# Denominators of odd tiles alone on POOL, the others by a square on ACT and a join on DVE, with a planner that keeps POOL and two-operand DVE passes apart

## The chip, the cores and the metric

The kernel runs on one core of a Trainium2 chip. The metric is the device time of one execution in microseconds (us). A core has a matrix engine (PE, with weight loads, PEld, beside it), a vector engine (DVE), an activation engine (ACT), a general engine (POOL) and a queue that issues transfers (SP). Each takes its instructions strictly in the order in which they were written, and waits for semaphores of the others.

## The reference, cut to what matters

Three layers follow each other on 4608 tokens (8 sequences of 576, 8 heads of 64 columns):

```python
p_packed = sm_attn(p, k, v)            # 32 packed rows for each head
x = sm_attn(q, p_packed, p_packed)     # 4608 x 512
h = x @ w_in                           # 512 -> 2048, call it layer 2
P = a[0] + a[1]*h + a[2]*h**2 + a[3]*h**3
Q = 1.0 + np.abs(b[0])*np.abs(h) + np.abs(b[1])*h**2
x = (P / (Q + 1e-6)) @ w_out           # 2048 -> 512
h = x @ w_in2                          # 512 -> 1024, layer 3
solu = h * softmax(h)
out = (layernorm(solu) * g_ln) @ w_out2  # 1024 -> 512
```

The change is about Q, the denominator of layer 2. Weights arrive as 64-bit floats and are turned into 32-bit ones on the chip.

## The kernel before, in words

The tokens go in nine blocks of 512 (j = 0 to 8). A block has 16 tiles of layer 2 (i = 0 to 15), each 128 of the 2048 columns by 512 tokens: `m_h` makes h in PSUM on PE, `elem` makes g = P/Q from it on ACT, POOL and DVE, and `m_y` multiplies g into four PSUM banks that collect the block's y. Blocks 0 and 1 (`NRAW = 2`) run these products in float32; from block 2 on all is split into a high and a low float16 half, with three passes for each product. `y_out` then splits y into `ybig`, and in four groups of 128 tokens `s_h2`, `s_sm`, `s_lt`, `s_ln` and `s_out` do layer 3.

`elem` of one tile, before: ACT takes u = |h| (L690), POOL makes s = |b1| u + |b0| (a tensor_scalar, shown under the helper's line L335 as `s<-u,aba`) and s = s u (a tensor_tensor, L692), so that s = Q - 1. ACT makes the start of P (L693), DVE two passes on it that read h from PSUM (L694, L695), ACT the logarithm and the exponential of s as a first reciprocal (L696, L697), DVE one Newton step and the product (L698, L699, and L701 in blocks 0 and 1 or L703 after). From block 2 on ACT rounds g to float16 (L704) and POOL makes the low half (L705, `g<-B,g`).

Ahead of this stands the start. `w_decode` turns 24 groups of weights into float32 with three DVE passes each (L399, L400, L401), ACT takes absolute values (L408) for bounds, PE sums those with a matrix of ones, and `w_split` (L457 on ACT, L458 on DVE) makes float16 halves. The attention of the next batch element runs between the tiles: `a_s1`, `a_tr`, `a_pp` (PE, with DVE's `p` pass, L332, behind it), `a_pt` (L518), `a_s2` and `a_pw`, which makes four groups of `pw` (PE into a pair of PSUM banks, ACT L538, DVE L539). The same pair of banks, the slot "S2", also serves `s_h2`, whose last reader is DVE's L757.

The order on every engine is made while the program is built. Each piece of work is a part of `plan` with an engine, a due time, a cost, and the keys that it reads and writes. `Plan.order` walks through a pretended execution: whenever an engine is free in it, the ready part with the earliest due time is taken, within `DUE["ahead"]` of the pace of the `m_h` parts. The due time of a part is 16 j + DUE[name] + offset, and a key (j, name) in `DUE` takes the place of the bare name. On the chip nothing of this clock is left: only each engine's order and the semaphores are.

## Time and profile before

| | before |
|---|---|
| median of 3 runs | 1197.74 us (1196.11 to 1203.66) |
| the profiled execution | 1202.27 us, its span 1200.4 us |
| PE busy | 1115.8 us, 93% |
| DVE busy | 976.8 us, 81% |
| ACT busy | 762.0 us, 63% |
| POOL busy | 706.3 us, 59% |
| TensorE clock granted, mean | 0.983 |

The span runs from the first to the last instruction. The busy time of an engine is the part of the span in which it has an instruction at work; register, branch and semaphore instructions don't count. An average over the span mixes a start, in which weights are decoded, with a long even stretch and an end, so the rows below are read by stretch.

### The profile page before, as it was taken

Reading aid. Unit: us, or ns where it says so; the run is one execution under the profiler, and the core shown is the slowest. Engines: PE = TensorE matmul, PEld = TensorE weight load, DVE = VectorE, ACT = ScalarE, POOL = GpSimd, SP = SyncE. Lnnn points to the kernel's source line nnn. Section 1 sums busy time; section 2 is a strip of 40 time slices with the busy share of each in tenths; the row PEclk is TensorE's granted clock in tenths of the full one; section 3 lists DMA queues with packets and bytes.
Section 4 is the critical chain, followed back from the end, with each engine's and each line's share of the span. In section 5 each row is a group of like instructions: output and inputs, shape, how many; then the busy total and the mean of one; then the engine's idle time right before and its main releaser. Section 6 shows DMA issues by size and latency. Waiting matters only on the chain.

```text
span 1200.4 us, 17951 instructions
## 1 busy us (share of the span) xinstructions
PE 1115.8 (93%) x6549; PEld 529.7 (44%) x6550; DVE 976.8 (81%) x1477; ACT 762.0 (63%) x1256; POOL 706.3 (59%) x931
## 2 busy tenths in 40 slices
PE   4678989999999999999999998999999999999998
PEld 1133344444444454444544454444444444444443
DVE  5987999999978978888878887888788886788633
ACT  3556666676856667567756766577656666667624
POOL 0163847554658647676666655765675865867612
PEclk9698999999999999999999999999999999999999
DMA  9664033110222121311231114111311121211123
GB/s 342 224 230 161 7 123 99 36 53 1 54 77 67 27 54 55 88 27 28 62 109 27 27 40 131 27 27 27 117 28 27 27 53 28 53 27 27 27 53 88
DMA packets 108120, 83.54 MB, mean 70 GB/s; under 512 B 78208, under 2 KB 88576, under 8 KB 108032
## 3 DMA queue, kind: packets, MB, share of 16 engines
q1 hardware_dynamic: 108032, 82.40, 24.4%
q8 instruction: 51, 0.84, 0.3%
q14 instruction: 37, 0.30, 0.1%
HBM read 54.07 MB, written 9.44 MB: 53 GB/s over the span
## 4 chain that ended last, share of the span: by engine, by line
PE 47%; DVE 23%; POOL 13%; ACT 9%; issue 5%; DMA 2%; SPq 0%; DVEq 0%; ACTq 0%; POOLq 0%
PE P L329 37%; PE h L329 9%; POOL s L692 4%; POOL cf L335 3%; DVE B L699 3%; POOL s L335 2%; DVE s L698 2%; POOL g L705 2%; ACT u L696 2%; DVE B L694 2%; DVE B L695 2%; POOL d L335 1%; DVE w L401 1%; DMA lbig<-lbig 1%; DVE at L629 1%
## 5 line engine op out<-in xcount | busy, mean ns | idle before, releaser
L329 PE MATMUL P<-g,w 128*128 128x512 f16 (+1 forms) x1600 | 423.4, 414 | 0.7 <-DVE ybig L729 0.7
L329 PE MATMUL h<-at,pw 128*128 128x192 f16 (+11 forms) x1408 | 235.4, 315 | 8.3 <-ACT at L646 3.2
L335 POOL TENSOR_SCALAR s<-u,aba 128x512 f32<-128x512 f32 x130 | 137.6, 1058 | 173.7 <-ACT u L690 150.9
L329 PEld LDWEIGHTS <-w 128*128 128x128 f16 x1440 | 138.4, 98 | 167.5 <-issue 12.1
L329 PE MATMUL P<-w,ybig 128*128 128x512 f16 x864 | 193.9, 381 | 9.0 <-DVE pw L539 2.5
L705 POOL TENSOR_TENSOR g<-B,g 128x512 f16<-128x512 f32 x112 | 144.2, 1287 | 80.9 <-ACT g L704 76.6
L692 POOL TENSOR_TENSOR s<-s,u 128x512 f32<-128x512 f32 x130 | 186.3, 1433 | 7.0
L329 PE MATMUL P<-w,lbig 128*128 128x512 f16 x768 | 173.0, 379 | 4.9 <-DVE pw L539 2.9
L335 POOL TENSOR_SCALAR d<-d 128x1 f32<-128x1 f32 x216 | 85.3, 395 | 156.6 <-ACT E L790 73.1
L696 ACT ACTIVATE u<-s,lnb 128x512 f32<-128x512 f32 x130 | 93.8, 721 | 98.4 <-POOL s L692 97.9
L698 DVE SCALAR_TENSOR_TENSOR s<-s,u 128x512 f32<-128x512 f32 x130 | 109.2, 840 | 47.8 <-ACT u L697 47.0
L329 PEld LDWEIGHTS <-ybig 128*128 128x128 f16 x864 | 84.7, 98 | 114.2 <-issue 16.0
L329 PEld LDWEIGHTS <-pw 128*128 128x128 f16 x1152 | 101.6, 98 | 64.5 <-issue 13.3
L329 PEld LDWEIGHTS <-lbig 128*128 128x128 f16 x768 | 74.6, 98 | 92.6 <-issue 8.1
L694 DVE SCALAR_TENSOR_TENSOR B<-h,cf,B 128x512 f32<-128x512 f32 x112 | 83.0, 741 | 27.5 <-ACT B L693 27.3
L693 ACT ACTIVATE B<-h,cf 128x512 f32<-128x512 f32 x112 | 86.6, 773 | 21.5 <-POOL g L705 21.5
L699 DVE SCALAR_TENSOR_TENSOR B<-B,cf,u 128x512 f32<-128x512 f32 x101 | 98.2, 972 | 0.0
L697 ACT ACTIVATE u<-u,lnb 128x512 f32<-128x512 f32 x133 | 95.6, 719 | 2.0
L690 ACT ACTIVATE u<-h,cf 128x512 f32<-128x512 f32 x101 | 68.9, 682 | 39.9 <-PE h L329 38.1
L695 DVE SCALAR_TENSOR_TENSOR B<-B,cf,h 128x512 f32<-128x512 f32 x112 | 82.8, 739 | 1.5
L704 ACT CAST g<-B 128x512 f16<-128x512 f32 x112 | 68.6, 613 | 21.6 <-PE P L329 16.9
L703 DVE SCALAR_TENSOR_TENSOR B<-s,B 128x512 f32<-128x512 f32 x98 | 81.0, 827 | 1.1
(144 smaller groups left out, 1469.3 us busy)
## 6 DMA issues: line engine op xcount, KB each, us to landing
w<-in_w_in_dram SPq DMA_DIRECT2D x10, 1024.0 KB, 9.2
kq<-in_kT_dram SPq DMA_DIRECT2D x8, 1152.0 KB, 6.2
w<-in_w_out_dram SPq DMA_DIRECT2D x9, 1024.0 KB, 8.1
kq<-in_qT_dram SPq DMA_DIRECT2D x9, 1024.0 KB, 5.4
out_dram<-w SPq DMA_DIRECT2D x36, 256.0 KB, 2.4
v<-in_vN_dram SPq DMA_DIRECT2D x15, 512.0 KB, 3.7
lbig<-in_w_out_dram SPq DMA_DIRECT2D x3, 1024.0 KB, 5.4
lbig<-in_w_in_dram SPq DMA_DIRECT2D x2, 1024.0 KB, 7.0
```

The costliest lines, as they stand in the source:

```text
L329: nc.tensor.matmul(out=o, lhsT=lhsT, rhs=rhs, start=start, stop=stop)
L335: gp.tensor_scalar(out=o, in0=i, scalar1=s1, scalar2=s2, op0=o0, **({"op1": o1} if o1 else {}))
L692: pool(due, c_pool(512, 2), lambda: gp.tensor_tensor(out=T(s_), in0=T(s_), in1=T(u_), op=ALU.mult), [u_, s_], [s_])
L693: sc(due, c_act(512, 163), lambda: act.activation(out=T(B_), in_=T(h_), func=AF.Identity, scale=coef(17), bias=coef(16)), [h_, *R], [B_], ...
L694: dve(due, c_dve(512), lambda: stt(out=T(B_), in0=T(h_), scalar=coef(14), in1=T(B_), op0=ALU.mult, op1=ALU.mult), [h_, B_, *R], [B_])
L695: dve(due, c_dve(512), lambda: stt(out=T(B_), in0=T(B_), scalar=coef(15), in1=T(h_), op0=ALU.subtract, op1=ALU.mult), [h_, B_, *R], [B_])
L696: sc(due, c_act(512, 105), lambda: act.activation(out=T(u_), in_=T(s_), func=AF.Ln, scale=2.0 ** -40, bias=lnb[:, 0:1]), [s_, "lnb"], [u_])
L697: sc(due, c_act(512, 105), lambda: act.activation(out=T(u_), in_=T(u_), func=AF.Exp, scale=-1.0, bias=lnb[:, 1:2]), [u_, "lnb"], [u_])
L698: dve(due, c_dve(512, 140), lambda: stt(out=T(s_), in0=T(s_), scalar=1.0 + 1e-6, in1=T(u_), op0=ALU.add, op1=ALU.mult), [s_, u_], [s_])
L699: dve(due, c_dve(512, 240), lambda: stt(out=T(B_), in0=T(B_), scalar=coef(18), in1=T(u_), op0=ALU.subtract, op1=ALU.mult), [B_, u_, *R], [B_])
L703: dve(due, c_dve(512, 95), lambda: stt(out=T(B_), in0=T(s_), scalar=2.0, in1=T(B_), op0=ALU.subtract, op1=ALU.mult), [s_, B_], [B_])
L705: pool(due, (1250, 1290), lambda: gp.tensor_tensor(out=T(g_)[:, 1, :], in0=T(B_), in1=T(g_)[:, 0, :], op=ALU.subtract), [B_, g_], [g_])
```

## The change: what it does

1. `elem` has two ways to Q. For odd tiles of blocks 2 to 8 (`Q_POOL`) all stays. For the other tiles (all 32 of blocks 0 and 1, and 56 of the later ones) ACT makes s = (c h)^2 and u = |b0 c h|, and one DVE pass joins them, s = |b1| s + u. The coefficient c b0 is a new small POOL instruction for each block (C(22)).
2. Parts on POOL, and DVE passes marked `port=True` (those with two operands in SBUF, and the decode's first), may not overlap in the pretended execution: while one of them is at work, `Plan.order` holds the others back. No semaphore is added for that.
3. Planner's costs: lower ones for POOL (`c_pool`, `SMALL_P`, L705's), and the extra time that some DVE passes had been given is taken out.
4. `DUE` gets due times for each group of loads and decodes (L00 to D33) and separate ones for blocks 0, 1 and 8, with new numbers everywhere; `ahead` goes from 14.05 to 25.54.

`LOW_POOL` is 0 for every matrix and `LO_POOL` is always true, so those two branches change nothing.

```diff
 DUE = {
-    "ahead": 14.05, "misc": -33.52, "L0": -86.47, "L1": 5.38, "D0": -129.29, "D1": -37.47, "L2": 15.2, "L3": -131.81, "D2": 27.27, "D3": 30.75,
+    "ahead": 25.54, "misc": -68.19, "S1": -126.89, "S2": -106.52, "S3": -44.43, "bound": -35.99, "mean": -76.81, "k": -7.86, "v": -59.3,
...
-    def add(self, eng, due, cost, fn, r=(), w=(), new=(), pace=None):
+    def add(self, eng, due, cost, fn, r=(), w=(), new=(), pace=None, port=False):
...
+        if port or eng == "POOL":
+            self.port.add(n)
...
                         due, n = heapq.heappop(heap)
+                        if n in self.port and port_at > now:
+                            held.append((due, n))
+                            continue
...
                     free_at[eng] = now + occ
+                    if got in self.port:
+                        port_at = now + occ
...
+    LOW_POOL = {1: 0, 2: 0, 3: 0}
+    Q_POOL = lambda j, i: j > 1 and i % 2
+    LO_POOL = lambda j, i: True
...
-        lat = (2.4 * n + 220) if tensors > 1 else (1.3 * n + 330)
+        lat = (2.14 * n + 175) if tensors > 1 else (0.94 * n + 290)
...
             steps += [("p", C(15), C(14), C(12), None, ALU.mult),
+                      ("p", C(22), C(14), abc[:, 4:5], None, ALU.mult),
...
-        sc(due, c_act(512, 65), lambda: act.activation(out=T(u_), in_=T(h_), func=AF.Abs, scale=coef(14)), [h_, *R], [u_], [(u_, "u"), (s_, "s")])
-        pool(due, c_pool(512), lambda: ps_(T(s_), T(u_), aba[:, 5:6], aba[:, 4:5], ALU.mult, ALU.add), [u_, "ab"], [s_])
-        pool(due, c_pool(512, 2), lambda: gp.tensor_tensor(out=T(s_), in0=T(s_), in1=T(u_), op=ALU.mult), [u_, s_], [s_])
+        if Q_POOL(j, i):
...
+        else:
+            sc(due, c_act(512, 65), lambda: act.activation(out=T(s_), in_=T(h_), func=AF.Square, scale=coef(14)), [h_, *R], [s_], [(s_, "s")])
+            sc(due, c_act(512, 65), lambda: act.activation(out=T(u_), in_=T(h_), func=AF.Abs, scale=coef(22)), [h_, *R], [u_], [(u_, "u")])
+            dve(due, c_dve(512), lambda: stt(out=T(s_), in0=T(s_), scalar=aba[:, 5:6], in1=T(u_), op0=ALU.mult, op1=ALU.add), [u_, s_, "ab"], [s_], port=True)
...
-        dve(due, c_dve(512, 140), lambda: stt(out=T(s_), in0=T(s_), scalar=1.0 + 1e-6, in1=T(u_), op0=ALU.add, op1=ALU.mult), [s_, u_], [s_])
+        dve(due, c_dve(512, 0), lambda: stt(out=T(s_), in0=T(s_), scalar=1.0 + 1e-6, in1=T(u_), op0=ALU.add, op1=ALU.mult), [s_, u_], [s_], port=True)
...
-            w_load(w, g, at(0, f"L{w}", g), places.get((w, g), lstage))
-            w_decode(w, g, at(0, f"D{w}", g))
+            w_load(w, g, at(0, f"L{w}{g}"), places.get((w, g), lstage))
+            w_decode(w, g, at(0, f"D{w}{g}"))
```

How the order moves is shown at four places. In the new program the lines of `elem` stand lower: the join is L725, and L694, L695, L698, L699, L701 and L703 have become L727, L728, L731, L732, L734 and L736; the decode's three are L422 to L424, DVE's `pw` pass is L566, and L332 and L335 are L355 and L358.

**POOL at the start of the program.** Before, its first work is the s of block 0's tiles, two passes each:

```order
L936 UNCONDITIONAL_BRANCH
L335 ISA
L335 TENSOR_SCALAR s_85<-u_87,aba 128x512
L692 TENSOR_TENSOR s_85<-s_85,u_87 128x512
L335 TENSOR_SCALAR s_86<-u_88,aba 128x512
L692 TENSOR_TENSOR s_86<-s_86,u_88 128x512
```

After, it is small passes for the scales of the weights (`wst`) and of the blocks (`cf`):

```order
L972 UNCONDITIONAL_BRANCH
L358 ISA
L358 TENSOR_SCALAR wst<-wst 128x1 x4
L358 TENSOR_SCALAR cf_117<-pmx 128x1
L358 TENSOR_SCALAR cf_117<-cf_117,wst 128x1
L358 TENSOR_SCALAR cf_117<-cf_117,aba 128x1 x2
L358 TENSOR_SCALAR cf_117<-cf_117 128x1
```

No pass over 128x512 stands on POOL any more until block 2.

**DVE among the first tiles of block 0**, where decodes (`w_74`, `w_75` from the staging places `w_76`, `w_77`) and tiles alternate. Before:

```order
L699 SCALAR_TENSOR_TENSOR B_91<-B_91,abc,u_87 128x512
L400 SCALAR_TENSOR_TENSOR w_74<-w_76,w_74 128x1024
L701 SCALAR_TENSOR_TENSOR g_92<-s_85,B_91 128x512
L401 SCALAR_TENSOR_TENSOR w_74<-w_76,w_74 128x1024
L399 TENSOR_SCALAR w_74<-w_76 128x1024
L698 SCALAR_TENSOR_TENSOR s_86<-s_86,u_88 128x512
L400 SCALAR_TENSOR_TENSOR w_74<-w_76,w_74 128x1024
L399 TENSOR_SCALAR w_75<-w_77 128x1024
L401 SCALAR_TENSOR_TENSOR w_74<-w_76,w_74 128x1024
L400 SCALAR_TENSOR_TENSOR w_75<-w_77,w_75 128x1024
L699 SCALAR_TENSOR_TENSOR B_89<-B_89,abc,u_88 128x512
L401 SCALAR_TENSOR_TENSOR w_75<-w_77,w_75 128x1024
```

After:

```order
L423 SCALAR_TENSOR_TENSOR w_74<-w_76,w_74 128x1024
L731 SCALAR_TENSOR_TENSOR s_86<-s_86,u_88 128x512
L424 SCALAR_TENSOR_TENSOR w_74<-w_76,w_74 128x1024
L422 TENSOR_SCALAR w_74<-w_76 128x1024
L732 SCALAR_TENSOR_TENSOR B_90<-B_90,abc,u_88 128x512
L423 SCALAR_TENSOR_TENSOR w_74<-w_76,w_74 128x1024
L734 SCALAR_TENSOR_TENSOR g_92<-s_86,B_90 128x512
L424 SCALAR_TENSOR_TENSOR w_74<-w_76,w_74 128x1024
L727 SCALAR_TENSOR_TENSOR B_91<-h_83,B_91 128x512
L731 SCALAR_TENSOR_TENSOR s_85<-s_85,u_87 128x512
L728 SCALAR_TENSOR_TENSOR B_91<-B_91,abc,h_83 128x512
L725 SCALAR_TENSOR_TENSOR s_86<-s_86,aba,u_88 128x512
```

The joins have come in among the tiles' passes; decodes and tiles still alternate.

**DVE at the second `p` pass of an attention in the later blocks**, for which PE's transpose L518 waits. Before:

```order
L695 SCALAR_TENSOR_TENSOR B_90<-B_90,cf_119,h_83 128x512
L698 SCALAR_TENSOR_TENSOR s_85<-s_85,u_87 128x512
L699 SCALAR_TENSOR_TENSOR B_90<-B_90,cf_119,u_87 128x512
L703 SCALAR_TENSOR_TENSOR B_90<-s_85,B_90 128x512
L332 TENSOR_SCALAR p_110<-P_82,sum_124 128x64
L520 TENSOR_REDUCE pm_126<-p_110 128x1
```

After:

```order
L728 SCALAR_TENSOR_TENSOR B_90<-B_90,cf_119,h_83 128x512
L736 SCALAR_TENSOR_TENSOR B_89<-s_85,B_89 128x512
L731 SCALAR_TENSOR_TENSOR s_86<-s_86,u_87 128x512
L355 TENSOR_SCALAR p_110<-P_82,sum_124 128x64
L547 TENSOR_REDUCE pm_126<-p_110 128x1
L732 SCALAR_TENSOR_TENSOR B_90<-B_90,cf_119,u_87 128x512
```

Two passes of the tile that stood ahead of `p` now stand behind it.

**DVE at the second `pw` group of the same attention.** Before, layer 3's group has used the pair of banks in between, and its L757 and a tile stand ahead:

```order
L757 SCALAR_TENSOR_TENSOR E_95,d_114<-P_82,d_114,E_95 128x1024
L787 RECIPROCAL d_114<-d_114 128x1
L694 SCALAR_TENSOR_TENSOR B_90<-h_83,cf_119,B_90 128x512
L695 SCALAR_TENSOR_TENSOR B_90<-B_90,cf_119,h_83 128x512
L698 SCALAR_TENSOR_TENSOR s_86<-s_86,u_88 128x512
L699 SCALAR_TENSOR_TENSOR B_89<-B_89,cf_119,u_88 128x512
L703 SCALAR_TENSOR_TENSOR B_89<-s_86,B_89 128x512
L539 SCALAR_TENSOR_TENSOR pw_104<-P_82,bnd,pw_104 128x2x512
```

After, one group follows another:

```order
L566 SCALAR_TENSOR_TENSOR pw_102<-P_82,bnd,pw_102 128x2x512
L355 TENSOR_SCALAR cf_117<-cf_117 128x1
L727 SCALAR_TENSOR_TENSOR B_90<-h_84,cf_119,B_90 128x512
L728 SCALAR_TENSOR_TENSOR B_90<-B_90,cf_119,h_84 128x512
L732 SCALAR_TENSOR_TENSOR B_89<-B_89,cf_119,u_87 128x512
L657 TENSOR_TENSOR at_100<-at_100,r_128 128x1024
L736 SCALAR_TENSOR_TENSOR B_89<-s_85,B_89 128x512
L566 SCALAR_TENSOR_TENSOR pw_103<-P_82,bnd,pw_103 128x2x512
```

On PE the three first groups of an attention now stand one tile (an h and a Y product) apart, ahead of any group of layer 3; before, groups of `pw` and of layer 3 took turns in the pair of banks.

## Rows read from the trace of the kernel before

**Rows 1.** Busy time by stretch of the span (us): start and end of the stretch, its length, then PE, PEld, DVE, ACT and POOL busy with the count of instructions, the granted TensorE clock (1 is 2.4 GHz), the busy share of the DMA engines, and GB/s.

```profile
0.00:19.00 19.00, 4.42 (x36) 1.27 (x36) 6.99 (x12) 4.16 (x6) 0.19 (x4) 1.00 0.93 329
19.00:303.00 284.00, 249.28 (x1198) 108.35 (x1200) 263.48 (x399) 181.22 (x323) 141.88 (x152) 0.93 0.33 113
30.00:60.00 30.00, 19.06 (x107) 5.92 (x103) 28.50 (x34) 17.24 (x32) 4.88 (x4) 0.62 0.63 224
303.00:970.00 667.00, 635.38 (x4226) 316.35 (x4225) 556.46 (x844) 441.34 (x711) 439.50 (x606) 1.00 0.21 53
970.00:1170.00 200.00, 200.00 (x970) 91.87 (x969) 139.19 (x204) 121.98 (x195) 117.80 (x143) 1.00 0.18 38
```

**Rows 2.** What PE waited for from 19 to 303 us, longest in total first: us in total, times, longest.

```profile
PE P L329 <- ACT pw L534: 9.5, 1, 9.5
PE P L329 <- ACT w L408: 6.0, 1, 6.0
...
PE h L329 <- ACT at L646: 3.2, 1, 3.2
PE P L358 <- DVE wst L425: 2.9, 1, 2.9
```

**Rows 3.** Instructions of POOL, DVE, ACT and PE from 77 to 97 us, in the order POOL, DVE, ACT, PE: start, duration (us), engine, line, what it writes and reads; in brackets the idle time of its engine just before it and what ended that.

```profile
77.41 10.88 POOL L335 TENSOR_SCALAR s<-u,aba 128x512 f32<-128x512 f32 x1 [3.73 <-DVE g L701]
...
78.29 0.69 DVE L399 TENSOR_SCALAR w<-w 128x1024 uint32<-128x1024 uint32 x1
...
87.65 0.67 DVE L694 SCALAR_TENSOR_TENSOR B<-h,B 128x512 f32<-128x512 f32 x1
96.35 0.28 DVE L332 TENSOR_SCALAR p<-P,sum 128x64 f32<-128x64 f32 x1 [8.02 <-PE P L329]
...
89.67 0.72 ACT L696 ACTIVATE u<-s,lnb 128x512 f32<-128x512 f32 x1 [10.12 <-POOL s L692]
...
93.13 0.59 PE L329 MATMUL P<-w,ones 128*32 128x512 bf16 x1 [9.54 <-ACT pw L534]
```

**Rows 4.** DVE's costliest groups from 19 to 303 us: line, operation, tiles, shapes, count; busy us and mean ns of one; idle us before them and what ended it.

```profile
L699 DVE SCALAR_TENSOR_TENSOR B<-B,abc,u 128x512 f32<-128x512 f32 x32 | 29.1, 910 | 0.0
L458 DVE SCALAR_TENSOR_TENSOR w<-w,wst 128x512 f16<-128x512 f32 x30 | 24.6, 826 | 0.0
L698 DVE SCALAR_TENSOR_TENSOR s<-s,u 128x512 f32<-128x512 f32 x32 | 23.8, 744 | 2.0 <-ACT u L697 1.8
L695 DVE SCALAR_TENSOR_TENSOR B<-B,abc,h 128x512 f32<-128x512 f32 x32 | 23.5, 733 | 0.8 <-ACT u L690 0.7
L701 DVE SCALAR_TENSOR_TENSOR g<-s,B 128x512 f32<-128x512 f32 x32 | 22.7, 709 | 0.0
L694 DVE SCALAR_TENSOR_TENSOR B<-h,B 128x512 f32<-128x512 f32 x32 | 21.6, 679 | 2.9 <-ACT B L693 2.5 <-ACT u L690 0.4
```

**Rows 5.** Groups of ACT from 19 to 303 us, columns as in rows 4.

```profile
L696 ACT ACTIVATE u<-s,lnb 128x512 f32<-128x512 f32 x33 | 23.7, 719 | 41.6 <-POOL s L692 41.6
...
L690 ACT ACTIVATE u<-h 128x512 f32<-128x512 f32 x32 | 18.7, 586 | 9.4 <-DVE B L695 4.2 <-PE h L329 3.5 <-DVE B L694 1.3
```

**Rows 6.** The two groups of POOL from 19 to 303 us that make s, columns as in rows 4.

```profile
L335 POOL TENSOR_SCALAR s<-u,aba 128x512 f32<-128x512 f32 x33 | 51.6, 1564 | 122.9 <-ACT u L690 102.9 <-DVE g L701 18.6 <-ACT d L793 0.9
L692 POOL TENSOR_TENSOR s<-s,u 128x512 f32<-128x512 f32 x33 | 51.0, 1546 | 2.4
```

**Rows 7.** The page's group of ACT's absolute value in the later blocks, columns as in rows 4, over the whole span.

```profile
L690 ACT ACTIVATE u<-h,cf 128x512 f32<-128x512 f32 x101 | 68.9, 682 | 39.9 <-PE h L329 38.1
```

**Rows 8.** What PE waited for from 303 to 970 us, as in rows 2.

```profile
PE P L329 <- DVE E L757: 5.7, 4, 2.8
PE P L518 <- DVE p L332: 5.7, 5, 1.6
PE P L329 <- DVE pw L539: 5.2, 6, 2.0
PE P L329 <- ACT E L490: 3.1, 3, 1.2
```

**Rows 9.** Instructions around a `p` pass at 605 to 612 us, of POOL, ACT, DVE and PE, columns as in rows 3.

```profile
605.41 1.83 POOL L692 TENSOR_TENSOR s<-s,u 128x512 f32<-128x512 f32 x1
...
607.27 0.72 ACT L696 ACTIVATE u<-s,lnb 128x512 f32<-128x512 f32 x1 [2.03 <-POOL s L692]
...
609.24 1.05 DVE L698 SCALAR_TENSOR_TENSOR s<-s,u 128x512 f32<-128x512 f32 x1 [2.47 <-ACT u L697]
610.21 0.74 DVE L699 SCALAR_TENSOR_TENSOR B<-B,cf,u 128x512 f32<-128x512 f32 x1
610.98 0.69 DVE L703 SCALAR_TENSOR_TENSOR B<-s,B 128x512 f32<-128x512 f32 x1
...
611.92 0.33 PE L518 MATMUL P<-idt,p 128*128 128x128 f32 x1 [1.65 <-DVE p L332]
```

**Rows 10.** PE's instructions behind a first `pw` group (619 to 626 us), and at a later one (784.83 us), columns as in rows 3.

```profile
619.22 1.09 PE L329 MATMUL P<-w,ppT 64*32 64x512 f32 x16
...
621.56 2.75 PE L329 MATMUL P<-g,w 128*128 128x512 f16 x12
624.88 1.46 PE L329 MATMUL P<-w,ybig 128*128 128x512 f16 x6 [0.57 <-DVE pw L539]
...
784.83 1.09 PE L329 MATMUL P<-w,ppT 64*32 64x512 f32 x16 [2.82 <-DVE E L757]
```

More of the change, by code (lines that the diff above doesn't have):

```diff
@@ L100, in order @@
                 heapq.heappush(ready[p[0]], (p[1], n))
-        out, now, events, pace = [], 0.0, [], 0.0
+        out, now, events, pace, port_at = [], 0.0, [], 0.0, 0.0
         bytes_free = 0.0
@@ L314, in pe, with dve @@
         plan.add("PE", due, c_pe(mms), run, r, w, new, pace)
-    def dve(due, cost, fn, r=(), w=(), new=()):
-        plan.add("DVE", due, cost, fn, r, w, new)
+    def dve(due, cost, fn, r=(), w=(), new=(), port=False):
+        plan.add("DVE", due, cost, fn, r, w, new, port=port)
     def sc(due, cost, fn, r=(), w=(), new=()):
@@ L457, in w_split @@
         sc(due, c_act(512, 100), lambda: act.activation(out=spl[w][:, c, 0, :], in_=raw[w][:, c + 1, :], func=AF.Copy, scale=s), [b, ("wst", w)], [a])
+        if LOW_POOL[w]:
+            sc(due, c_act(512, 100), lambda: act.activation(out=raw[w][:, c + 1, :], in_=raw[w][:, c + 1, :], func=AF.Copy, scale=s), [b, ("wst", w), a], [b])
+            pool(due, (1117, 1157), lambda: gp.tensor_tensor(out=spl[w][:, c, 1, :], in0=raw[w][:, c + 1, :], in1=spl[w][:, c, 0, :], op=ALU.subtract), [a, b], [a, ("spl", w, c)])
+            return
         dve(due, c_dve(512), lambda: v_.scalar_tensor_tensor(out=spl[w][:, c, 1, :], in0=raw[w][:, c + 1, :], scalar=s, in1=spl[w][:, c, 0, :], op0=ALU.mult, op1=ALU.subtract),
-            [a, b, ("wst", w)], [a, ("spl", w, c)])
+            [a, b, ("wst", w)], [a, ("spl", w, c)], port=True)
     def load_k(b, due):
@@ L774, in s_lt @@
         sc(due, c_act(1024, 20), lambda: act.activation(out=l[:, 0, 0, :], in_=T(E), func=AF.Copy, scale=2.0 ** 13), [E], [R, *old])
-        dve(due, c_dve(1024, 0), lambda: v_.scalar_tensor_tensor(out=l[:, 0, 1, :], in0=T(E), scalar=2.0 ** 13, in1=l[:, 0, 0, :], op0=ALU.mult, op1=ALU.subtract), [E, R], [(R, 1)])
+        dve(due, c_dve(1024, 0), lambda: v_.scalar_tensor_tensor(out=l[:, 0, 1, :], in0=T(E), scalar=2.0 ** 13, in1=l[:, 0, 0, :], op0=ALU.mult, op1=ALU.subtract), [E, R], [(R, 1)], port=True)
         for a in range(2):
```

36 lines of the change are left out of this document (21 added, 15 removed), and 18 rows, old and new, of the table DUE.

## The prediction, made before the changed kernel ran

> **What bounds the kernel now.** I read the busy times by stretch first, then in each stretch the waits of the engine that has least room, then the instructions around the longest waits. The stretches differ [rows 1]. Up to 19 us everything waits for transfers: PE works 4.4 us and DVE 7.0. From 19 to 303 us (blocks 0 and 1, the decodes and splits) DVE is at work for 263.5 of 284 us and PE for 249.3, so both are near full and DVE is the fuller one. From 303 to 970 us PE works 635.4 of 667 us and DVE only 556.5: here PE sets the pace and the 31.6 us in which it stands still are all that a better order can win. From 970 to 1170 us PE works 200.00 of 200 us and nothing can be won. The end, 30 us, has 3.7 us without PE (the span's total less the stretches before), and its last products and transfer are the same after the change.
>
> The waits say what PE stands still for. In the start one wait of 9.5 us and one of 6.0 lead [rows 2]. The first is a chain [rows 3]: a POOL pass that makes s began at 77.41 us and took 10.88 us, while DVE ran its passes back to back from before 78.29 until 88.3 us; ACT waited 10.12 us for s, the `pw` copy stood behind that on ACT, PE waited 9.54 us behind the copy, and in the end DVE itself stood still for 8.02 us. Later the waits are short and belong to the attention: 5.7 us for L757 ahead of `pw` groups, 5.7 us for `p`, 5.2 us for DVE's `pw` pass, 3.1 us for L490 [rows 8].
>
> **The change part by part. The start, 19 to 303 us.** As many decodes, splits, tiles and PE products stand ahead of the last float32 g in the new order as in the old, within some 2 us of PE's work, so the order moves nothing out of this stretch. What counts is DVE's sum.
>
> Added: 32 joins. The nearest row is L701, a pass over the same shape with both operands in SBUF in the same stretch: 22.7 us for 32 [rows 4]. The ends are 21.6 us, the fastest group of 32 there (L694), and 29.1 us, the most stretched one (L699). Successive passes start some 0.08 us before the one ahead has ended (in rows 3 the pass of 87.65 us, 0.67 long, closes a run without gaps), so I take 22.7 less 32 x 0.08, that is +20.
>
> Taken away: DVE's 8.02 us wait [rows 3], since no tile of blocks 0 and 1 has a pass on POOL any more: -8. And DVE's stretching by POOL: passes with one operand in PSUM hold steady (L694 679 ns, L695 733 ns) while those with two in SBUF don't (L699 910 ns) [rows 4]. Against L695 for L699 and L458, and L694 for L698 and L701, the excess is 5.6 + 2.6 (24.6 less 30 x 0.733) + 2.2 + 1.1 = 11.5 us. POOL's two groups of s, 51.6 + 51.0 us at 1564 and 1546 ns a pass [rows 6], are nearly all of POOL's 141.9 us there [rows 1]; what stays on POOL is small passes. I take -10.
>
> The trace thus shows that POOL and two-operand passes hold each other up, and that a POOL pass can stay shut out through a whole run of them. The Trainium skill (SBUF — State Buffer, "Who interferes with whom") has a lock for it: a DVE pass with two SBUF inputs and a GpSimd pass that reads SBUF exclude each other, and whichever starts first keeps the shared port for its whole length. The stretched L699 beside the steady L695 agrees; by that rule the small passes left on POOL could not stretch much, and the sum of the start would be 1.5 us lower (all of the 11.5 us back). The 10.88 us don't agree, since by the rule POOL would get its turn after one DVE pass of at most 1.2 us.
>
> The chain of a tile gets shorter as well: two POOL passes of 1.56 and 1.55 us [rows 6] give way to one ACT pass of 0.586 us [rows 5] and a join of 0.7. ACT waited 41.6 us in this stretch for s [rows 5]. DVE's short waits that hang on it (2.0 and 2.9 us in rows 4) can lose half: -2. The bounds for this are 0 and -5. ACT's 32 further passes (32 x 0.586 = 18.8 us) lie in its 103 free us [rows 1]; if they delayed h's readers instead, the price is 0.59 us for a tile, some +4 us at worst where PE's next h waits for the bank.
>
> POOL's chains for the blocks' scales (`cf`), no longer queued behind passes of s, are ready earlier; nothing waits for them long enough to count. The 6.0 us wait for L408 and the 3.2 us for L646 [rows 2], at 37 to 50 us, lie in the first attention, whose DVE work the new order leaves in place, so they stay, and with them the clock of 0.62 from 30 to 60 us [rows 1], a stretch that for most of its length had the lower level of 1.2 GHz; PE had stood still in it for 11 us.
>
> Sum of the start on DVE: +20 - 8 - 10 - 2 = 0. PE's own share comes on top: its longest wait is 1.5 us longer than DVE's, and of its 2.9 us for the weights' scale (L425) [rows 2], a DVE pass that stands among the tiles' passes, I count half: -3. Bounds: -9 (21.6 - 2.6 - 8 - 11.5 - 5 - 3) to +12 (22.7 without overlap, less 8 and 6, and ACT's delays of h with 4).
>
> **The later blocks, 303 to 970 us.** DVE gets 8 joins for each block, 56 in all; ACT 56 passes at 0.682 us [rows 7]; POOL loses 112 passes. DVE's and ACT's additions, some 5.6 us and 5.5 us for each block, lie in the free 110.5 us and 225.7 us of this stretch [rows 1]. So the sum is one of waits of PE.
>
> `pw`: the three first groups now stand together, so they no longer wait for layer 3's L757: -5.7 [rows 8]. In its place comes the wait of a `pw` group for the one before it. Its price is the row with the same cover, one h and one Y product, before the next user of the banks: 0.57 us [rows 10]. It occurred about once in a block and would now occur three times; two more in six blocks are 12 x 0.57 = +6.8 at most, and 0 if DVE gets to its pass sooner. Between two such passes on DVE stand six others that add up to some 4 us, about as long as PE's cover, so I take two thirds, +4.5.
>
> `p`: PE's 1.65 us wait at 610 us was DVE's [rows 9]. POOL's s took 1.83 us, ACT waited 2.03 us for it, DVE 2.47 us, and then L699 (0.74) and L703 (0.69) still ran before `p`. Both now stand behind `p`, so each such wait loses 1.4 us. The five `p` waits of 5.7 us [rows 8] hold three of that size: -4.
>
> The rest (L490, L627 and smaller, some 15 us) hangs on when DVE and ACT get to the attention's passes. Shorter s chains help in every second tile, and a denser DVE hurts. I take a third, -5, bounds -10 and +6.
>
> Sum: -5.7 + 4.5 - 4 - 5 = -10. Bounds: -20 (-5.7 - 4 - 10, no new `pw` wait) to +9 (-5.7 + 6.8 + 6, and `p` back at 2).
>
> **The end, 970 us on.** PE has no idle time, and keeps its products: 0.
>
> **Rivals.** First, the keeping apart holds only in the plan. No wait enforces it, so on the chip POOL and DVE drift into each other as before, and the denser DVE eats what the order wins: the start at -3, the later blocks at 0, which gives 1195, within 1%. For it: POOL keeps 56 x 2 passes of s and 112 low halves, and DVE gets more two-operand passes. Against it: `p` and `pw` are moved in the order itself.
>
> Second, slower: DVE becomes the bound of the start beyond what it gets back. Place: the run of decodes and tiles from 60 to 303 us, where DVE had hardly a gap but the 8.0 us. If joins cost 22.7 us without overlap, the remaining POOL work stretches DVE as before, and the shorter chain helps nothing, the start is +22.7 - 8 = +14.7 and the later blocks 0: 1212. It decides as soon as less than about 5 us of the 11.5 us of stretching come back. For it: DVE is at 93% in the stretch. Against it: the passes of s that did the stretching are gone there.
>
> Third, by the skill's lock, a POOL pass can't be shut out for longer than one DVE pass, so the 10.88 us would have another cause and could come again under another name: the start at +5 instead of -3, the later blocks at -10, that is 1193. The rows speak against it: POOL's pass ends within 0.1 us of DVE's run.
>
> Fourth, the new due times do more than these rows let me price (a due time for each decode, others for blocks 0 and 1): the start at -9 with 3 more for the first attention, the later blocks at -20, that is 1166. For it: 34.7 us of PE's idle time lie in the start and 31.6 in the later blocks. Against it: DVE's sum.
>
> **How the numbers follow.** On the profiled execution (span 1200.4, time 1202.3) the sum is -3 - 10 = -13, so 1189.3. The median of the runs lies 4.5 us below the profiled time: 1197.7 - 13 = 1185 us. Chances: forecast 0.42, first rival 0.25, second 0.12, third 0.04, fourth 0.17. A measurement of this kernel tells a difference from none at about 1%, or 12 us. Faster by over 1% (below 1186) takes the fourth, somewhat more than half of the forecast's spread (1174 to 1195), and a little of the first: 0.17 + 0.25 + 0.06 = 0.48. Slower by over 1% is most of the second: 0.10. Within 1%: 0.42. The range of 1163 to 1205 holds the forecast, the first and third and most of the fourth, and leaves out the second.
>
> **What would show it right or wrong.** After: no POOL pass over 128x512 before block 2, none of some 10 us, and L696 no longer waiting 41.6 us; L699's first 32 passes at about 735 ns; PE idle from 19 us to the last float32 g near 33 us, that g near 301 us; L757 gone from PE's waits ahead of `pw`, the `pw` waits more in number; `p` waits below 0.5 us. Wrong: joins of over 0.8 us, DVE without a gap and that g at 310 us or later; or PE's idle time in the later blocks unchanged at 30 us, with new names.

## The result and the profile after

The changed kernel takes 1159.62 us (median of 4 runs, 1156.36 to 1161.38) against 1200.2 us before on the same chip: a ratio of 0.966, 95% interval 0.9616 to 0.9704. The forecast of 1185 us had the sign right and the size wrong; 1159.6 lies below its range. The profiled execution took 1156.4 us, its span is 1154.5 us. Its busy time by stretch, columns as in [rows 1]:

```profile
19.00:303.00 284.00, 262.09 (x1310) 115.47 (x1298) 271.23 (x441) 211.76 (x375) 54.82 (x101) 0.96 0.35 118
303.00:970.00 667.00, 660.30 (x4379) 330.43 (x4378) 562.87 (x911) 474.12 (x779) 377.26 (x540) 1.00 0.22 54
970.00:1154.50 184.50, 179.91 (x861) 81.32 (x859) 129.75 (x201) 113.78 (x185) 77.33 (x117) 1.00 0.18 41
```

And two stretches of the start, the same columns:

```profile
30.00:60.00 30.00, 17.20 (x119) 5.73 (x119) 28.09 (x36) 17.56 (x33) 0.00 (x0) 0.72 0.63 226
...
90.00:120.00 30.00, 29.90 (x150) 10.75 (x144) 29.43 (x53) 23.77 (x39) 12.41 (x26) 1.00 0.39 132
```

PE works 660.3 of the 667 us between 303 and 970 us, where it worked 635.4 [rows 1]: nearly all that could be won there is won. In the same 284 us of the start it works 12.8 us more, and the granted clock from 30 to 60 us is 0.72 instead of 0.62. What PE still waits for, first from 19 to 303 us, then from 303 to 970 us (us in total, times, longest):

```profile
PE P L352 <- ACT w L431: 6.8, 1, 6.8
PE P L352 <- DVE g L734: 3.4, 1, 3.4
PE h L352 <- ACT at L674: 3.2, 1, 3.2
```

```profile
PE P L545 <- DVE p L355: 2.5, 5, 1.0
PE P L381 <- ACT ppT L546: 1.8, 5, 0.4
PE P L352 <- DVE E L793: 1.2, 3, 0.5
```

The 9.5 us wait of [rows 2] is gone; the first attention's two stayed (now L431 and L674). In the later blocks the waits for `pw` and L490 have vanished, `p` fell from 5.7 to 2.5 us, and L793 (before L757) from 5.7 to 1.2 us [rows 8]. DVE's groups from 19 to 303 us, columns as in [rows 4], and ACT's wait for s there:

```profile
L485 DVE SCALAR_TENSOR_TENSOR w<-w,wst 128x512 f16<-128x512 f32 x32 | 23.7, 743 | 0.0
L725 DVE SCALAR_TENSOR_TENSOR s<-s,aba,u 128x512 f32<-128x512 f32 x31 | 23.0, 742 | 1.1 <-ACT u L724 1.1
L732 DVE SCALAR_TENSOR_TENSOR B<-B,abc,u 128x512 f32<-128x512 f32 x30 | 22.3, 742 | 0.0
```

```profile
ACT u L729 <- DVE s L725: 8.1, 8, 3.2
```

A pass of L732 takes 742 ns, where L699 took 910 [rows 4], a join takes 742 ns (0.7 us were taken), and ACT waits 8.1 us for s instead of 41.6 [rows 5].

### The profile page after: what moved, and what is told of

Read it like the earlier page. It is cut to its first block, busy times and chain, and to the rows that moved or that the text cites. A ratio compares the mean times of both kernels' runs of the same rounds, so it can differ in the third digit from the quotient of the medians.

```text
span 1154.5 us, 17857 instructions
## 1 busy us (share of the span) xinstructions
PE 1104.5 (96%) x6550; PEld 527.9 (46%) x6550; DVE 973.6 (84%) x1565; ACT 804.1 (70%) x1344; POOL 509.6 (44%) x762
## 4 chain that ended last, share of the span: by engine, by line
PE 70%; DVE 16%; ACT 9%; issue 3%; DMA 1%; SPq 1%; POOL 0%; ACTq 0%; DVEq 0%; POOLq 0%
PE P L352 54%; PE h L352 14%; DVE B L732 3%; DVE s L731 2%; DVE B L727 2%; ACT B L726 1%; DVE B L728 1%; DVE w L424 1%; ACT u L729 1%; DVE B L736 1%; DMA kq<-in_kT_dram 1%; ACT u L730 1%; DVE s L725 1%; ACT u L724 1%; DVE w L423 1%
## 5 line engine op out<-in xcount | busy, mean ns | idle before, releaser
L358 POOL TENSOR_SCALAR d<-d 128x1 f32<-128x1 f32 x216 | 100.7, 466 | 236.0 <-ACT E L788 96.4
L739 POOL TENSOR_TENSOR g<-B,g 128x512 f16<-128x512 f32 x112 | 140.3, 1253 | 127.3 <-ACT g L737 122.5
L729 ACT ACTIVATE u<-s,lnb 128x512 f32<-128x512 f32 x127 | 91.8, 723 | 38.6 <-DVE s L725 20.2
L731 DVE SCALAR_TENSOR_TENSOR s<-s,u 128x512 f32<-128x512 f32 x127 | 97.9, 771 | 23.0 <-ACT u L730 20.8
L730 ACT ACTIVATE u<-u,lnb 128x512 f32<-128x512 f32 x138 | 99.5, 721 | 1.9
L727 DVE SCALAR_TENSOR_TENSOR B<-h,cf,B 128x512 f32<-128x512 f32 x112 | 83.0, 742 | 17.6 <-ACT B L726 17.2
L732 DVE SCALAR_TENSOR_TENSOR B<-B,cf,u 128x512 f32<-128x512 f32 x108 | 89.1, 825 | 0.0
L728 DVE SCALAR_TENSOR_TENSOR B<-B,cf,h 128x512 f32<-128x512 f32 x112 | 83.0, 742 | 2.4
L788 ACT ACTIVATE E<-P,d,cf 128x1024 f32<-128x1024 f32 x36 | 43.2, 1201 | 53.5 <-DVE d L355 53.5
L352 PEld LDWEIGHTS P<-g,w 128*128 128x128 f32 x256 | 47.8, 191 | 60.3 <-issue 54.0
L786 DVE TENSOR_REDUCE d<-P 128x1 f32<-128x1024 f32 x36 | 43.9, 1220 | 33.8 <-PE P L352 33.7
L358 POOL TENSOR_SCALAR wst<-wst 128x1 f32<-128x1 f32 x8 | 2.6, 322 | 154.0 <-DVE wst L382 149.5
```

Of the source, the lines that this page charges most:

```text
L352: nc.tensor.matmul(out=o, lhsT=lhsT, rhs=rhs, start=start, stop=stop)
L358: gp.tensor_scalar(out=o, in0=i, scalar1=s1, scalar2=s2, op0=o0, **({"op1": o1} if o1 else {}))
L727: dve(due, c_dve(512), lambda: stt(out=T(B_), in0=T(h_), scalar=coef(14), in1=T(B_), op0=ALU.mult, op1=ALU.mult), [h_, B_, *R], [B_])
L728: dve(due, c_dve(512), lambda: stt(out=T(B_), in0=T(B_), scalar=coef(15), in1=T(h_), op0=ALU.subtract, op1=ALU.mult), [h_, B_, *R], [B_])
L729: sc(due, c_act(512, 105), lambda: act.activation(out=T(u_), in_=T(s_), func=AF.Ln, scale=2.0 ** -40, bias=lnb[:, 0:1]), [s_, "lnb"], [u_])
L730: sc(due, c_act(512, 105), lambda: act.activation(out=T(u_), in_=T(u_), func=AF.Exp, scale=-1.0, bias=lnb[:, 1:2]), [u_, "lnb"], [u_])
```

## The experiments

All ratios are to the kernel before on the same chip, which took 1200 to 1204 us. **Denominators** old means that POOL makes s for every tile. **Order** says where an engine's order comes from: kept means that only the instructions of one part are exchanged in an order made for others, planned that the planner made it anew. The planner's costs (point 3 of the change) are the old ones in e1, e7, e8 and e11 and the new ones in all other runs.

| run | denominators | due times | port rule | order | us | ratio |
|---|---|---|---|---|---|---|
| before | old | old | off | | 1200 to 1204 | 1 |
| after | new | new | on | | 1159.6 | 0.966 |
| e1 | new | old | off | kept, before's | 1198.0 | 0.996 |
| e2 | old | new | on | kept, after's | 1196.1 | 0.994 |
| e3 | old in blocks 0, 1 | new | on | kept, after's | 1174.9 | 0.977 |
| e4 | old | new | on | planned | 1185.9 | 0.986 |
| e5 | new | new | off | planned | 1213.4 | 1.012 |
| e6 | new | old, one moved | on | planned | 1172.8 | 0.978 |
| e7 | new | old, one moved | off | planned | 1198.7 | 0.999 |
| e8 | old | old, one moved | off | planned | 1215.0 | 1.012 |
| e9 | new | old | on | planned | 1179.1 | 0.981 |
| e10 | new | old | off | planned | 1216.2 | 1.012 |
| e11 | old | old, one moved | on | planned | 1213.0 | 1.009 |

The intervals are 0.1 to 0.5% to either side. In e6 and e7 the absolute value of a few tiles can be issued before its buffer is free, so that these tiles come out wrong; e9 and e10 tie it to the square, and it stands behind that.

**Which part brings the time: e1 to e4.** The exchange in e1, and the reverse one in e2 (for all tiles) and e3 (`back = j < 2`):

```diff
 e1, in before's parts
+        def den():   # POOL's tiles: the old absolute value
+            act.activation(out=T(s_), in_=T(h_), func=AF.Square, scale=coef(14))
+            act.activation(out=T(u_), in_=T(h_), func=AF.Abs, scale=coef(22))
+        def den2():  # in the place of POOL's second pass
+            stt(out=T(s_), in0=T(s_), scalar=aba[:, 5:6], in1=T(u_), op0=ALU.mult, op1=ALU.add)
 e2, in after's join
+            ps_(T(s_), T(u_), aba[:, 5:6], aba[:, 4:5], ALU.mult, ALU.add)
+            gp.tensor_tensor(out=T(s_), in0=T(s_), in1=T(u_), op=ALU.mult)
 e4
-    Q_POOL = lambda j, i: j > 1 and i % 2
+    Q_POOL = lambda j, i: True
```

> The kernel before, in its own order of instructions, with only the denominators changed: where a tile is not an odd one of a later block, ACT makes a square and an absolute value in the old absolute value's place, and the join stands on DVE where POOL's second pass was issued. All due times, costs and the port rule stay as before. Theory A (the passes: what is won is POOL's long passes of s that no longer stretch DVE's passes and shut each other out, and the shorter chain of a tile): most of the 41 us come with this alone, 1160 to 1175 us. Theory B (the order: the new due times and the port rule put the work where it is not waited for, and the passes only add DVE work): little comes, 1185 to 1205 us. Theory C (both together: the joins need an order that has room for them, and the order needs the short chains): 1175 to 1190 us here, and the other half in the opposite experiment.

> The changed kernel, in its own order of instructions, with the old denominators: no square, the absolute value by ACT, and POOL's two passes issued where the join stood, for every tile. Theory A (the passes): nearly all of the gain is lost, 1185 to 1205 us, POOL's 128x512 passes are shut out by DVE for over 5 us at the worst, and DVE's passes are again stretched by some 100 us over the run (before 106, after 46). Theory B (the order): 1155 to 1172 us, since DVE loses 68 us of joins and the order stays. Theory C (both): 1172 to 1190 us.

> As the experiment on the old denominators in the changed kernel's order, but only for blocks 0 and 1; the later blocks keep the joins. Theory A: the last float32 g comes at 300 us or later (before 303.4, after 290.3), DVE's excess by stretching up to there is back near 19 us (after 2.3), and the whole takes 1170 to 1176 us; the later blocks stay as in the changed kernel. Theory B: that g stays within 3 us of 290 us, and the whole within 4 us of 1160, since 23 us of joins leave DVE and 19 us of stretching come back.

> The changed kernel with POOL making s for every tile, and the order planned anew with the new due times, costs and the port rule. Theory A: 1185 to 1205 us; the port rule can keep POOL and DVE apart only by leaving one of them idle, so DVE's stretching is smaller than before but its idle time larger. Theory B: 1155 to 1175 us. Theory C: 1172 to 1190 us. Due times that were chosen for other passes may also cost some us by themselves; the first two experiments, which keep an order, are free of that.

e1 falls into Theory B's range, e2 and e3 into Theory A's, e4 into A's and C's: neither part does much without the other. That is Theory C, and stronger than I had put it. The passes in the old order bring 0.4%, the new order with the old denominators 0.6% (1.4% when it is planned for them, e4), both 3.4%. The stretch from 303 to 970 us and PE's longest waits in it, first e1, then e2 (lines are a little shifted: L540 is DVE's `pw` pass, L776 and L800 are layer 3's pass that was L757, L855 is ACT's pass that was L812):

```profile
303.00:970.00 667.00, 635.58 (x4200) 315.64 (x4199) 563.60 (x883) 463.96 (x752) 337.91 (x522) 0.99 0.20 52
```

```profile
PE P L330 <- DVE pw L540: 10.4, 12, 2.8
PE P L330 <- DVE E L776: 3.3, 3, 1.3
```

```profile
303.00:970.00 667.00, 647.92 (x4282) 322.65 (x4281) 545.03 (x848) 442.60 (x719) 462.86 (x616) 1.00 0.22 53
```

```profile
PE P L352 <- DVE E L800: 7.9, 11, 1.6
PE P L352 <- ACT w L855: 3.3, 4, 1.1
```

In e1 PE works there as little as before (635.6 and 635.4 us): with the old order the new denominators gain nothing in the later blocks, and PE's waits for the attention stay. All that e1 gains, 5 us, lies in the start: its last float32 g ends at 298.8 us, before 303.4. In e2 the order gains half of the later blocks, but ACT waits there for POOL's second pass of s (54.0 us from 303 to 970 us), and waits for layer 3 stand in place of those for `pw`. e3 keeps the later blocks as after and loses 0.011 of 1200 us, some 13 us, in the start (PE works 660.3 us from 303 to 970 us in both); its last float32 g ends at 309.4 us, after's at 290.3. So one and the same exchange in the start is worth 5 us in the old order and 13 in the new. e4, planned for its own passes, is as fast as after from block 2's end to block 6's (414 to 875 us, after 409 to 869), and loses some 25 us at blocks 7 and 8, where three waits, 13.1 us together, stand within 20 us:

```profile
1029.44 2.72 PE L352 MATMUL h<-at,pw 128*128 128x512 f16 x6 [3.84 <-DVE B L728]
1036.71 2.72 PE L352 MATMUL h<-at,pw 128*128 128x512 f16 x6 [4.55 <-DVE B L728]
1044.19 2.31 PE L352 MATMUL P<-w,ybig 128*128 128x512 f16 x5 [4.75 <-ACT ybig L764]
```

From block 2 to block 6 the new denominators are thus not needed for the gain, provided that the order is planned for the old ones; in blocks 7 and 8 e4 does not show that.

**Due times or port rule: e5 to e11.** In e5, e7 and e10 the rule is off; in e6, e7, e9 and e10 the old table stands in `DUE`; e7 is the kernel before, old costs included, with the new denominators planned in; e8 and e11 are the kernel before without and with the rule. The lines that count:

```diff
-                        if n in self.port and port_at > now:
+                        if False and n in self.port and port_at > now:
 e6, e7, e8, e11, in the old table
-    "D2": 27.27
+    "D2": 19.27
```

> The changed kernel with the rule off that keeps POOL and two-operand DVE passes apart in the plan; denominators, due times and costs are the new ones. Theory P (the keeping apart carries the order's part): DVE's stretching over the run grows from 46 towards 80 us or more, PE waits come back, 1175 to 1195 us. Theory D (the due times carry it): the order differs only in details, 1155 to 1168 us, and the stretching rises by some 10 to 20 us that lie in DVE's free time.

> The changed kernel (new denominators, port rule, new costs) planned with the old due times; only layer 2's decode is due 8 units earlier than in the old table, since the plan has no order without that. Theory D (the due times): the later blocks keep their waits for `pw`, L793 and `p`, PE's idle time from 303 to 970 us stays near 30 us, 1185 to 1202 us. Theory P (the keeping apart): 1158 to 1175 us.

> The kernel before with the new denominators, planned anew with the old due times and costs and without the port rule (layer 2's decode due 8 units earlier). The first experiment had them in the old order at 1198 us, 5 us below before. If that order, made for other passes, kept their gain back, the new plan gives 1175 to 1188 us. If the due times are what is missing, 1190 to 1203 us.

> A control: the kernel before with nothing changed but layer 2's decode due 8 units earlier, as in the two experiments with old due times. Both theories expect 1197 to 1208 us, within 5 us of before; a larger difference would show how much one due time does by itself, and would widen what those two can tell.

> The changed kernel with new denominators, port rule and new costs, planned with exactly the old due times; the square claims both buffers of a tile and the absolute value is issued behind it. The experiment with old due times and layer 2's decode 8 units earlier took 1172.8 us. Theory P (the keeping apart in the plan is worth some 25 us, whatever the due times): 1165 to 1182 us. Theory K (all of these orders sit on a knife's edge, and any change of a due time moves the time by 10 us and more either way): anything between 1160 and 1200, over 8 us away from 1172.8.

> As the one with exactly the old due times, but the port rule off; denominators and costs are the new ones. Theory P: 1192 to 1205 us, some 25 us above it, with DVE's stretching 15 us or more larger. Theory K: the rule's worth has no fixed sign, within 8 us of it or below it.

> The kernel before (old denominators, old due times, old costs) with only the port rule added, and layer 2's decode due 8 units earlier as in the control, which took 1215.0 us without the rule. Theory P: 1185 to 1200 us. Theory J (the rule needs the joins: with 144 pairs of POOL passes it can keep them apart only by leaving DVE idle): 1205 to 1225 us, with DVE's idle time larger than in the control and its stretching smaller.

Theory P holds with the new denominators and costs: the rule alone is worth 37 us with the old due times (e10 to e9) and 54 with the new ones (e5 to after), more than P said (e5 and e10 lie above its ranges). With the old denominators, due times and costs it is worth 2 us (e8 to e11), Theory J; whether it lacks the new denominators there or the new costs, e11 does not tell. From e9 to after, where the new due times come in and the tie to the square goes, it is another 19 us. Theory K has something to it as well: one due time moved by 8 units costs the kernel before 12 us (e8, above what either theory allowed), and e6, with that one moved and without the tie, is 6 us faster than e9. Differences of that size between planned orders say little.

One rival stays open: the planner's new costs were not tried by themselves. From e7 to e6, 26 us, costs and rule come in together. And without the rule e7, with the old costs, takes 1198.7 us and e10, with the new ones, 1216.2 (the one due time and the tie differ as well), so a part of what the rule wins can be what the new costs lose without it.

The stretch from 303 to 970 us, PE's longest waits (for e9 also that for `pw`) and ACT's wait for POOL's s in it, e9 (rule on), then e10 (off). Their lines stand 12 above those of after (L716 is L728, L717 L729, L709 L721, L554 L566, L781 L793); POOL's helper line is L346:

```profile
303.00:970.00 667.00, 651.96 (x4333) 324.41 (x4332) 572.84 (x908) 478.15 (x772) 355.91 (x538) 1.00 0.21 53
```

```profile
PE h L340 <- DVE B L716: 3.3, 4, 1.3
...
PE P L340 <- DVE pw L554: 0.5, 1, 0.5
```

```profile
ACT u L717 <- POOL s L709: 21.4, 23, 3.3
```

```profile
303.00:970.00 667.00, 621.01 (x4131) 308.34 (x4130) 553.56 (x862) 455.61 (x737) 343.64 (x508) 0.99 0.20 51
```

```profile
PE P L340 <- DVE pw L554: 11.1, 12, 1.9
PE P L340 <- DVE E L781: 9.4, 8, 2.3
```

```profile
ACT u L717 <- POOL s L709: 52.3, 26, 7.3
```

The rule gives PE 31 us here, and the wait for `pw` falls from 11.1 us to 0.5. How much of that is less contention? The engines' line of the page (busy, share, instructions; it is DVE and POOL that count), e9, then e10:

```profile
PE 1109.6 (94%) x6549; PEld 529.1 (45%) x6550; DVE 980.8 (83%) x1565; ACT 812.9 (69%) x1344; POOL 483.3 (41%) x762
```

```profile
PE 1117.9 (92%) x6549; PEld 528.8 (44%) x6550; DVE 991.6 (82%) x1565; ACT 812.6 (67%) x1344; POOL 487.5 (40%) x762
```

For the same passes DVE is busy 11 us less with the rule and POOL 4, while the time falls by 37 us. The 7.3 us wait for s comes from POOL's order, as rows of e10 show (start, us, engine, line; idle before and its releaser in brackets):

```profile
632.52 0.77 POOL L346 TENSOR_SCALAR s<-u,aba 128x512 f32<-128x512 f32 x1
633.27 0.28 POOL L346 TENSOR_SCALAR cf<-bnd 128x1 f32<-128x1 f32 x1
...
637.16 1.16 POOL L727 TENSOR_TENSOR g<-B,g 128x512 f16<-128x512 f32 x1
...
638.60 1.26 POOL L709 TENSOR_TENSOR s<-s,u 128x512 f32<-128x512 f32 x1
...
639.90 0.72 ACT L717 ACTIVATE u<-s,lnb 128x512 f32<-128x512 f32 x1 [7.24 <-POOL s L709]
640.53 1.19 ACT L776 ACTIVATE E<-P,d,cf 128x1024 f32<-128x1024 f32 x1
...
643.19 1.09 PE L340 MATMUL P<-w,ppT 64*32 64x512 f32 x16 [1.13 <-DVE E L781]
```

Between POOL's two passes of one s stand ten small ones and a low half. ACT waits for s, layer 3's exponential stands behind it, DVE's L781 behind that, and PE waits for the banks. The same 7.24 us come back 125 and 250 us later: it is in the order, not an accident of the run.

e8 and e11 say the same from the other side. The same line of the page, e8, then e11:

```profile
PE 1122.3 (92%) x6549; PEld 532.3 (44%) x6550; DVE 973.9 (80%) x1477; ACT 762.2 (63%) x1256; POOL 715.5 (59%) x931
```

```profile
PE 1124.9 (93%) x6549; PEld 532.9 (44%) x6550; DVE 949.4 (78%) x1477; ACT 763.9 (63%) x1256; POOL 693.5 (57%) x931
```

For the same passes the rule takes 24 us from DVE's busy time and 22 from POOL's, and the time stays. As the order differs too, this shows that less stretching is not enough, not that it is worth nothing.

**How full DVE is in the start: e12.**

```diff
-            dve(due, c_dve(512, 0), lambda: stt(out=flat(T(g_)).bitcast(F32), ...), [s_, B_], [g_], [(g_, "g")], port=True)
+            dve(due, c_dve(512, 0), lambda: [stt(out=flat(T(g_)).bitcast(F32), ...) for _ in range(2)], [s_, B_], [g_], [(g_, "g")], port=True)
```

> The changed kernel in its own order, but in blocks 0 and 1 the last pass of each tile on DVE, which makes the float32 g, is made twice (the same result), 32 further passes of some 0.7 us, 22.7 us. Theory F (DVE is full in the start, as its 28.8 to 30.0 us of work in each 30 us say, so what is added there shows in full): 1176 to 1184 us, the last float32 g at 307 to 312 us (290.3 in the changed kernel). Theory R (there is room in DVE's gaps and PE sets the pace): below 1168 us.

1176.11 us, ratio 0.978, within Theory F's range. The last float32 g ends at 312.8 us (290.3 in the changed kernel): up to there the 22 us show in full. Of the whole time 15 us are left (0.0124 of 1200); how the rest is won back behind that g stays open. The doubled group, columns as in [rows 4]:

```profile
L734 DVE SCALAR_TENSOR_TENSOR g<-s,B 128x512 f32<-128x512 f32 x64 | 44.0, 687 | 2.4 <-PE P L352 1.2
```

**How the rule works: e13, e16, e17, e18.** In e13 the order of e10 is kept and the odd tiles get the join in the place of POOL's second pass, as in e1. The others have half of the rule; e16:

```diff
-                        if n in self.port and port_at > now:
+                        if n in self.port and eng == "DVE" and port_at > now:
...
-                    if got in self.port:
+                    if got in self.port and eng == "POOL":
```

e17 and e18 have the two engines' names exchanged.

> The order planned with the old due times and without the port rule, which took 1216.2 us, kept as it is; but the odd tiles of later blocks too get a square and an absolute value from ACT and a join on DVE where POOL's second pass was issued, so POOL makes no s at all. It adds 56 DVE passes of some 0.74 us, 41 us. Theory S (POOL's passes are shut out while DVE's two-operand passes run, and what stands behind them waits): 1180 to 1200 us, ACT's 63.3 us of waits for POOL's s are gone, and PE's idle time from 303 to 970 us falls from 46 to below 30 us. Theory O (that order puts the attention's passes too late, whatever POOL does): 1210 to 1235 us, with PE's waits for `pw` and L781 (25.8 us together) as large as before or larger, since DVE gets fuller.

> The changed kernel with half of the port rule: in the plan DVE's marked passes wait while a POOL pass is at work, POOL's passes start whenever they can. Whole rule 1159.6 us, none 1213.4 us. Theory V (the worth is that DVE's unmarked passes, `pw`, L793 and the reductions, go ahead of marked ones): 1158 to 1180 us, with PE's waits for L793 and `pw` nearly gone in the later blocks. Theory W (the worth is POOL's passes being moved away): 1195 to 1220 us.

> The changed kernel with the other half: in the plan POOL's passes wait while a marked DVE pass is at work, DVE's start whenever they can. Theory V: 1195 to 1220 us, PE's waits for L793 (14.4 us without the rule) and `pw` stay. Theory W: 1158 to 1180 us. Theory B (both halves are needed, since the due times were chosen with the whole rule): both runs at 1185 to 1215 us.

> The half in which POOL gives way, with exactly the old due times, where the whole rule took 1179.1 and none 1216.2 us. Theory V: 1200 to 1220 us. Theory W: 1172 to 1190 us.

e13 takes 1213.1 us (e10 1216.2): Theory O. No s is on POOL any more, and PE works 623.4 us in the later blocks instead of 621.0, with the same waits:

```profile
303.00:970.00 667.00, 623.42 (x4134) 309.51 (x4133) 571.72 (x907) 480.40 (x781) 238.54 (x425) 0.99 0.20 51
```

```profile
PE P L340 <- DVE pw L554: 12.7, 13, 1.4
PE P L340 <- DVE E L784: 8.0, 8, 2.8
```

So taking POOL's s away does not repair an order that was made without the rule (though 41 us of joins went into DVE). e16 takes 1184.1 us, e17 1206.6 and e18 1191.1. With the new due times DVE's giving way brings 29 of the 54 us and POOL's 7; with the old ones POOL's brings 25 of 37. The half in which DVE gives way was not run with the old due times. Neither V nor W holds alone: e16 and e18 lie between their ranges. Theory B, that both halves are needed, comes nearest. PE's wait for L793 from 303 to 970 us follows: 14.4 us without the rule, 11.7 in e17, 6.1 in e16, 1.2 with both. Which displaced passes carry the time stays open.

**Can it be made faster: e14, e15.** `LOW_POOL = {1: 1, ...}` and `{2: 1, ...}`:

> The changed kernel, planned anew, but the low halves of the second weight matrix are made by ACT (scaling in place) and POOL instead of DVE: 16 DVE passes of 0.743 us, 11.9 us, leave DVE in the start, and POOL, which has little to do there, gets 16 passes of some 1.16 us. If DVE's fullness in the start counts with 0.73 us for each us, as the doubled pass showed, 1148 to 1154 us. If POOL's passes stretch DVE's or are shut out, or the order comes out worse (a single other due time moved the kernel before by 12 us), 1158 to 1175 us.

> As the last, but for the third weight matrix (8 passes, 5.9 us, of which nearly all lie before the last float32 g). With 0.73 us for each us: 1153 to 1158 us. Otherwise 1158 to 1172 us.

1165.75 us (ratio 0.968) and 1162.91 us (0.9665): no gain over after's 0.966 beyond what the runs can tell. In e14 the last float32 g ends at 290.3 us, as in after: what left DVE was not won. A part of it went into stretching: up to that g, L732, L725 and L731 take 773, 770 and 713 ns in the mean of 30 passes each, where they take 742, 742 and 680 in the changed kernel, some 3 us of the 11.9.

## Why the prediction was wrong

**The steps that failed.** The prediction priced the passes as the change and the order as a remainder, and in both stretches the gain lies past its bound. In the later blocks it put PE's idle time at -10 us with a bound of -20, and that time fell by 24.9, from 31.6 to 6.7 us [rows 1]. By its own terms (us):

| PE's waits, 303 to 970 us | foretold | before | after | measured |
|---|---|---|---|---|
| L757 (now L793) | -5.7 | 5.7 | 1.2 | -4.5 |
| DVE's `pw` pass | +4.5 | 5.2 | 0 | -5.2 |
| `p` in L518 (now L545) | -4 | 5.7 | 2.5 | -3.2 |
| the rest | -5 | 15.0 | 3.0 | -12.0 |

Two steps failed there. "In its place comes the wait of a `pw` group for the one before it" is off by 9.7 us: that wait did not come, and those that there were went. DVE ends its pass 0.4 to 1.6 us before PE's next group starts, the closest time so:

```profile
477.35 1.28 DVE L566 SCALAR_TENSOR_TENSOR pw<-P,bnd,pw 128x1024 f16<-128x1024 f32 x1
...
479.02 1.09 PE L352 MATMUL P<-w,ppT 64*32 64x512 f32 x16
```

And "The rest (L490, L627 and smaller, some 15 us) hangs on when DVE and ACT get to the attention's passes ... I take a third, -5, bounds -10 and +6" is off by 7.0. What the runs show in their place is the planned order. The waits for `pw` are 10.4 us with the new denominators in the old order (e1), 11.1 planned without the rule (e10) and 0.5 with it (e9), and e2 and e4 gain in this stretch without the new denominators, e1 not at all with them. Which displaced passes carry the rest stays open. L757 came out near its price by luck: only two of its four waits, 0.96 and 2.82 us, stood ahead of `pw` groups.

In the start the step that failed is "so the order moves nothing out of this stretch. What counts is DVE's sum": -3 was foretold with a bound of -9, and the last float32 g came 13.1 us earlier. With the passes alone, in the old order, it came 4.6 us earlier (e1), so for these the sum was good. The order brought the other 8.5 us, most of it as idle time of DVE: up to that g some 32 us before, 25 in e1 and 18 in the changed kernel.

**Why the bound was too tight.** The first rival let the chip undo the rule, and nothing priced the rule as a way to another order. From e10 to e9 contention falls by far less than the time, and e13, with no s on POOL at all, stays at 1213 us. This speaks for the order that comes out of the plan, which was worth 37 and 54 us with the new denominators and costs. The fourth rival, 1166 us, had the size but named the due times alone, which bring 19.

**The start, term by term,** to the last float32 g, 303.4 us before and 290.3 after (-13, predicted -3). The same passes stand ahead of it in both, within one or two, as was said. DVE's durations to that g add up to 297.1 us before and 304.5 after. Against the first quartile of each shape, stretching was 19.4 and is 2.4 us: 17 came back, not 10; I had counted four groups and not the decodes and the small ones. The joins cost 23.7 us (32 x 742 ns), 22.7 were taken. Successive passes overlap by 32.7 us where they overlapped by 26.8, 5.9 more, not 2.6. DVE's idle time fell by 14.6 us, not 10. That is 23.7 - 17.0 - 5.9 - 14.6 = -13.8, and other passes +0.7. PE's -3 on top did not exist apart from these.

**What neither term holds.** The profiled spans differ by 45.9 us. That g accounts for 13.1 of them and PE's idle time in the later blocks for 24.9; the end gives 0.9 back. The other 8.8 us are PE's work: when that g ends, 852.9 us of it are left, before 861.7. The prediction, with as much work ahead of that g in either order "within some 2 us of PE's work", has no term for that.

**The clock.** I left the clock as it was. From 30 to 60 us it rose from 0.62 to 0.72 and from 90 to 120 us from 0.88 to 1.00, where PE had stood still for 9.54 us just before [rows 3]. Before, it stood at the lower level of 1.2 GHz for 37.7 us ahead of that g (28.8 to 35.7, 39.1 to 56.2, 86.9 to 97.1 and 131.2 to 134.7 us), after for 20.5 (39.1 to 56.2 and 63.0 to 66.4). The stretch around the wait at 93 us went with the wait. For the others that is not shown, since this is one execution of each, and the mean granted clock of the changed kernel's four executions alone runs from 0.985 to 0.991, the profiled one at the top. By the medians the gain is 40.6 us, not 45.9. PE's busy time fell by 11.3 us in the profiled ones; how much of that is the clock's stays open.

**What held.** No POOL pass over 128x512 in the start and none near 10 us, L699's successor at 742 ns (735 said), `p` down by 3.2 us (4 said, though its longest wait is 1.0 us and not below 0.5), L757 gone ahead of `pw`. The second rival's ground was true (DVE works 271.2 of the 284 us in the start, and e12 shows that it counts), but the stretching that came back and the idle time that went paid for it.

## What to carry to other kernels

Where a planner sets the order, try its parts one by one and together before pricing one: here the denominators in the old order brought 0.4%, the new order with the old denominators 0.6% (1.4% planned for them), and all together 3.4%. The planner's costs are such a part too, and want a run of their own. Bound an order's worth by all of the pacing engine's idle time (66 us here), not by the waits that one can name. And run a control with one due time moved: it cost 12 us here, so a smaller gap between two planned orders does not show a mechanism by itself.
